# One tile of x on another DMA queue, and the bias of the hidden layer loaded and transposed earlier, in a fused linear-attention and MLP block

## The chip, the cores and the metric

The kernel runs on one core of one Trainium2 chip. The metric is device time in microseconds, the median of three runs. The names used for the core's engines are those of the profile: PE (TensorE, the matmuls) with PEld (its weight loads), DVE (VectorE), ACT (ScalarE), POOL (GpSimd) and SP (SyncE). SP does no arithmetic here: it only issues DMA transfers. ACT issues a few too, from the same instruction stream that holds its activations. "ACTq" and "SPq" mark such issues in the profile.

## The reference

The input x has 2048 tokens of 448 features. The output is x + s * g. Both factors start from the same layer norm of x:

```python
xn = _layernorm(x, axis=-1)
# linear attention, 16 heads of 28
q, k, v = split(xn @ wqkv)
phi = lambda t: jnp.where(t > 0, t + 1, jnp.exp(t)) + 1e-6
pq, pk = phi(q), phi(k)
kv = einsum("bhsd,bhse->bhde", pk, v);  z = sum over s of pk
o = (pq @ kv) / (pq . z + 1e-6)
s = o @ wo
# dense part, 448 -> 1792 -> 448
h = xn @ w1 + b1
h = relu(h) ** 2
g = silu(h @ w2 + b2)
out = x + s * g
```

All matrices are bfloat16. b1 has 1792 entries, one for each hidden unit; it is added before the relu.

## The kernel before

**Tiling.** The tokens are 16 tiles of 128, in four groups of 512. For the hidden layer the 1792 units are 14 blocks of 128: each block gives a 128 x 512 result for one group of tokens, with units on partitions, so b1 is needed with one unit per partition: a 128 x 14 tile (`b1f`). It is loaded as 14 rows of 128 (`b1r`, 3.5 KB), transposed on PE against an identity and copied out of PSUM by ACT with an ordinary activation (`bias_cols`, L1235 to L1241). The contraction length 448 is cut into three pieces of 128 and one of 64 ("rest"); the rests of two tiles or blocks share the array as halves of 64 rows.

**The order of work.** The program lists operations with what they read and write. PE and SP keep the order of the list. For ACT, DVE and POOL a planner (`one_pass`, L98) picks the next operation with durations that stand beside each operation and due times worked out from PE's order. Where a transfer has an entry in the table `landing` (L1275) the planner takes its landing time from there. The table changes no instruction by itself: it only feeds the planner, which then orders ACT, DVE and POOL for the whole program and hands out the eight PSUM banks. Semaphore waits follow from the data. Two chains of `behind` (L1264 to L1274) fix the order of the first operations on DVE (statistics of tile 0, statistics of tile 1, normalization of tile 0, and so on) and on ACT (`rs1 eT0.0 ln2 eT1.0 rs2 ln3 rs3 b1f`). An operation with a lower `prio` number is due earlier.

**The head** is the first 10 us, for token tiles 0 to 3. In words, with the names that the prediction uses:

- SP issues, in this order: x0 (tile 0 of x, L453), x1 (L454), x23 (tiles 2 and 3 together, L455), the main part of the key weights ("wk main", L456), three loads for the first 256 hidden units (w10: main and two rests, L459 to L461), b1r (L462), then the three loads of the next hidden units (w11), tiles 4 and 5 of x, w12 and so on.
- ACT first loads its function table (L452). Then it issues the two rests of the key weights ("wk rests", L457 and L458), which are made to wait for the table.
- DVE takes bn_stats and bn_aggr of a tile (L497, L498); ACT makes 1/sqrt(var + eps) out of that with Ln and Exp (L505, L509); DVE normalizes (L527, called xn0, xn1 and so on below).
- PE first multiplies a tile of zeros (`warm`, L1217, "dummies": their results are not read). It then transposes the three whole pieces of tile 0 (T0, L1246, by the code at L604), runs five dummies (L1247), transposes tile 1 (T1, L1248), two more dummies, the rests of tiles 0 and 1 (TR0, L1250), and goes on to the keys of tiles 0 and 1 (K0, K1, L803, first reader of wk main), T2, the key rests (Kr0, L818, first reader of the wk rests), T3, the first hidden blocks (L831), the rests of tiles 2 and 3 (TR2, L1258), the bias transpose (B1, L1261), and the hidden blocks' rests (Hr0, L847).
- From then on PE runs the stream of L1367 to L1383 to the end.

Of the kernel before, what the change touches and what calls it, by code (L numbers as in the profile page):

```python
# [9 lines left out]
P = 128  # L10
S, D, F = 2048, 448, 1792
# [35 lines left out]
class Program:  # L47
# [6 lines left out]
    def add(self, eng, emit, reads=(), writes=(), dur=0.2, alts=(), nbytes=0, mode=None, label="", slow=1.0):  # L54
        op = Op(eng, emit, reads, writes, dur, alts, nbytes, mode, label)
        op.slow, op.behind, op.at = slow, None, None
        for t in op.reads:
            op.raw.add(self.writer[t])
            self.readers.setdefault(t, []).append(op)
        for t in op.writes:  # L60
            w = self.writer.get(t)
            if w is not None and w is not op:
                op.deps.add(w)
            for r in self.readers.get(t, ()):
                if r is not op:
                    op.deps.add(r)
            self.writer[t] = op
            self.readers[t] = [r for r in self.readers.get(t, ()) if r is op]
        op.raw.discard(op)
        op.deps |= op.raw  # L70
        for d in op.deps:
            d.succ.append(op)
        self.ops.append(op)
        return op
# [233 lines left out]
def bass_recurrent_scan__linear_attn_block__dense_activation_squared_relu__prompt_kernel(  # L308
    nc, A_x, A_wqkv, A_wo, B_x, B_w1, B_b1, B_w2, B_b2, out
):  # L310
    with ExitStack() as es:
# [14 lines left out]
        x_tok = sb("x_tok", [P, NT, D], bf)  # L326
# [9 lines left out]
        b1r = sb("b1r", [NF, P], bf)  # L336
# [83 lines left out]
        def tiles(t, lo, hi):  # L420
            if hi <= 2:
                return t[0][P * lo : P * hi].rearrange("(p s) d -> p s d", s=1)
            base, n = (2, 2) if hi <= 4 else (lo // 4 * 4, 4)
            v = t[0][P * base : P * (base + n)].rearrange("(p s) d -> p s d", s=n)
            return v[:, lo - base : hi - base, :]

        def dma(eng, dst, src, writes, nbytes, reads=(), dur=0.45, slow=1.0):
            return add(
                eng, lambda e, _: e.dma_start(dst, src), reads, writes, dur, nbytes=nbytes, label="dma" + str(writes[0]), slow=slow
            )  # L430

        def load_x(lo, hi, eng="sp"):
            dma(eng, x_tok[:, lo:hi, :], tiles(A_x, lo, hi), [("x", i) for i in range(lo, hi)], (hi - lo) * P * D * 2)

        def load_main(eng, w, src, name, lo, hi, c0=0, c1=3, off=0):
            dma(
                eng, w[:, c0:c1, lo:hi],
                src[128 * c0 : 128 * c1, off + lo : off + hi].rearrange("(c p) j -> p c j", p=P),
                [(name, c) for c in range(c0, c1)], 128 * (c1 - c0) * (hi - lo) * 2,
            )  # L440

        def load_rest(eng, w, src, name, lo, hi, off=0, part=None):
            for i in (0, 1) if part is None else (part,):
                dma(
                    eng, w[64 * i : 64 * i + 64, 3, lo:hi], src[384:448, off + lo : off + hi], [(name, 3 + i)],
                    64 * (hi - lo) * 2, ["actw"] if eng == "act" else (), dur=0.58,
                )
# [3 lines left out]
        cuts = (0, 2 * P, 6 * P, 10 * P, F)  # L451
        add("act", lambda e, _: e.preload_act_table_set("natural_log_exp_and_others"), [], ["actw"], 1.25, label="table").prio = -1e6  # L452
        load_x(0, 1, "sp")  # L453
        load_x(1, 2, "sp")  # L454
        load_x(2, 4, "sp")  # L455
        load_main("sp", w_k, A_wqkv, "wk", 0, D, off=D)  # L456
        load_rest("act", w_k, A_wqkv, "wk", 0, D, off=D, part=0)  # L457
        load_rest("act", w_k, A_wqkv, "wk", 0, D, off=D, part=1)  # L458
        load_main("sp", w_1, B_w1, "w10", cuts[0], cuts[1])  # L459
        load_rest("sp", w_1, B_w1, "w10", cuts[0], cuts[1], part=0)  # L460
        load_rest("sp", w_1, B_w1, "w10", cuts[0], cuts[1], part=1)  # L461
        dma("sp", b1r[:, :], B_b1.rearrange("(f p) -> f p", p=P), ["b1r"], F * 2)  # L462
        for i in (1, 2, 3):
            name = f"w1{i}"
            if i == 2:
# [156 lines left out]
        def pe_transpose_rests(lo, eng):  # L622
            b = Buf("T")

            def f(e, _):
                v = ps(b)[:, :].bitcast(bf)
                for i in range(2):
                    last = e.transpose(v[:, i * P : (i + 1) * P], xn[:, lo + i, 384:512], ident[:, :])
                return last

            ts = (lo, lo + 1)
            add("pe", f, [("xd", i) for i in ts] + ["ident"], [b], 0.0558 * 2, mode="128", label=f"TR{lo}")

            def ev(e, eng):
                src = ps(b)[:, 0:P].bitcast(bf).rearrange("p (t k) -> p t k", t=2)
                if eng == "dve":
                    return e.tensor_copy(xT[:, lo : lo + 2, 3, :], src)
                return e.activation(out=xT[:, lo : lo + 2, 3, :], in_=src, func=AF.Copy)

            add(eng, ev, [b], [("xT", i) for i in ts], 0.39 if eng == "act" else 0.25, label=f"eTR{lo}").prio = -30  # L640
# [187 lines left out]
        def head_part(lo, fi):  # L828
            def f(e, _):
                for c in range(3):  # L830
                    last = e.matmul(  # L831
                        ps(head[fi])[:, lo * P : (lo + 2) * P], w_1[:, c, fi * P : (fi + 1) * P], xT[:, lo : lo + 2, c, :],
                        start=(lo == 0 and c == 0), stop=False, skip_group_check=True,
                    )
                return last

            add(
                "pe", f, [("w10", c) for c in range(3)] + [("xT", lo + i, c) for i in (0, 1) for c in range(3)] + ([head[fi]] if lo else []),
                [head[fi]], 3 * MM(256), mode="128", label=f"Ha{fi}.{lo}",
            )  # L840

        def head_rest(lo):
            fs = (lo, lo + 1)

            def f(e, _):
                for h, fi in enumerate(fs):
                    last = e.matmul(  # L847
                        ps(head[fi])[:, 0:512], w_1[half[h], 3, fi * P : (fi + 1) * P], xT[half[h], 0:4, 3, :], start=False,
                        stop=True, skip_group_check=True,
                    )  # L850
                return last

            bs = [head[fi] for fi in fs]
            add("pe", f, [("xT", i) for i in range(4)] + [("w10", 3), ("w10", 4)] + bs, bs, MM(512), mode="64", label=f"Hr{lo}")
            for fi in fs:
                h_out(head[fi], 0, fi)
# [360 lines left out]
        def warm(n, after=(), src=None):  # L1217
            b = Buf("W")

            def f(e, _):  # L1220
                last = None
                for _i in range(n):
                    last = e.matmul(ps(b)[:, 0:P], src or dum[:, 0:P], src or dum[:, 0:P], start=True, stop=True)
                return last

            add("pe", f, ["dum", *after] if src is None else [], [b], n * 0.107, mode="128", label="warm")
# [8 lines left out]
        def bias_cols():  # L1235
            bb = Buf("B1")
            add(
                "pe", lambda e, _: e.transpose(ps(bb)[:, 0 : NF // 2].bitcast(bf), b1r[:, :], ident[0:NF, 0:NF]),
                ["b1r", "ident"], [bb], 0.1, mode="128", label="B1",
            )  # L1240
            add("act", lambda e, _: e.activation(out=b1f[:, :], in_=ps(bb)[:, 0 : NF // 2].bitcast(bf), func=AF.Copy), [bb], ["b1f"], 0.2, label="b1f")  # L1241
# [2 lines left out]
        warm(30)  # L1244
        warm(4, [("mv", 0)])
        pe_transpose(0, ((0, 3, "act"),))  # L1246
        warm(5)  # L1247
        pe_transpose(1, ((0, 3, "act"),))  # L1248
        warm(2)
        pe_transpose_rests(0, "dve")  # L1250
# [3 lines left out]
        k_rests(0)  # L1254
        pe_transpose(3, ((0, 3, "dve"),))
        head_part(0, 0)
        head_part(0, 1)
        pe_transpose_rests(2, "dve")  # L1258
        head_part(2, 0)
        head_part(2, 1)  # L1260
        bias_cols()  # L1261
        head_rest(0)

        byname = {op.label: op for op in pr.ops}  # L1264
        for first, order in (
# [7 lines left out]
            if first < -26:  # L1273
                byname[names[0]].prio = first  # L1274
        landing = {  # L1275
            ("x", 0): 2.8, ("x", 1): 3.45, ("x", 2): 4.45, ("wk", 0): 6.2, ("wk", 3): 6.1, ("wk", 4): 7.6, ("w10", 0): 7.25,
            ("w10", 3): 7.55, ("w10", 4): 7.75, ("b1r", None): 7.95, ("w11", 0): 8.95, ("w11", 3): 9.2, ("w11", 4): 9.45, ("x", 4): 9.9,
            ("w12", 0): 11.2, ("w12", 3): 11.4, ("w12", 4): 11.9, ("x", 6): 13.0, ("w13", 0): 14.5, ("w13", 3): 14.8, ("w13", 4): 15.0,
        }
        for (name, k), t in landing.items():  # L1280
# [136 lines left out]
```

## Time and profile before

| What | Value |
|---|---|
| median of 3 runs | 143.62 us (143.43, 143.62, 144.87) |
| the profiled execution, its own time | 142.37 us |
| its span | 141.1 us |
| PE busy | 137.6 us, 97% of the span |
| DVE / ACT / POOL busy | 104.0 / 77.4 / 6.3 us |
| first transfer of x issued; last matmul ends | 0.81 us; 138.6 us |
| DMA engines, mean busy share in stretches of 2 us from 2 to 10 us | 0.95, 1.07, 0.92, 0.89 |

The profile is of one execution. Its span counts from the first instruction of the program to the last, and its own time is 1.27 us more. Both are below the three timed runs, so differences are worked out against the profiled execution and then carried to the median. "Busy" of PE is modelled, since matmuls are pipelined; where PE's pace matters, starts of matmuls are compared. Landing times of transfers are the last of the semaphore updates that the trace holds for a transfer.

### The profile page before, as it was taken

What the parts mean: (1) busy time and instruction counts of PE and PEld (TensorE: products, weight loads), DVE (VectorE), ACT (ScalarE), POOL (GpSimd) and SP (SyncE); (2) the same over time, 40 slices, a digit from 0 to 9 for tenths busy, and PEclk for the clock granted to TensorE, in tenths of its full rate; (3) what the DMA queues carried; (4) which work ended last, traced back from release to release, by engine and by line L of the source; (5) the groups of instructions that cost most, each with busy time, mean ns of one, the idle gap of its engine ahead of it and who ended that gap; (6) DMA issues with size and microseconds to landing.
All of it is one profiled execution on the core that took longest, in us unless ns stands there. A gap on an engine that the chain in (4) does not pass through costs nothing.

```text
span 141.1 us, 3239 instructions
## 1 busy us (share of the span) xinstructions
PE 137.6 (97%) x1299; PEld 70.9 (50%) x1299; DVE 104.0 (74%) x226; ACT 77.4 (55%) x142; POOL 6.3 (4%) x40
## 2 busy tenths in 40 slices
PE   7999999999999999999999999999999999999992
PEld 7764445454444544444444444435447455555472
DVE  1988992999798898878867799695036516874875
ACT  3759993141988526986952867696138630301312
POOL 7900000000000000000000000000000000000000
PEclk9999999999999999999999999999999999999999
DMA  4999997249923000323000000000796001223033
GB/s 98 277 289 293 312 327 147 40 61 299 178 41 52 5 0 6 50 42 47 12 5 0 0 0 5 0 0 19 183 211 133 0 0 35 96 69 102 33 98 98
DMA packets 24220, 12.91 MB, mean 91 GB/s; under 512 B 14354, under 2 KB 23566, under 8 KB 24206
## 3 DMA queue, kind: packets, MB, share of 16 engines
q1 hardware_dynamic: 22414, 11.35, 31.9%
q10 hardware_dynamic: 1792, 1.36, 4.3%
q8 instruction: 10, 0.16, 0.5%
q14 instruction: 4, 0.03, 0.1%
HBM read 9.23 MB, written 1.90 MB: 79 GB/s over the span
## 4 chain that ended last, share of the span: by engine, by line
PE 93%; DVE 3%; DMA 1%; issue 0%
PE pb L788 29%; PE pb L1094 23%; PE pb L1186 8%; PE pb L889 7%; PE pb L731 7%; PE pb L741 6%; PE pb L1111 4%; PE pb L1151 3%; DMA x_tok<-in_A_x_dram 1%; PE pb L868 1%; DVE st L497 1%; DVE gbuf L1175 1%; PE pb L895 1%; PE pb L831 1%; PE pb L1038 1%; PE pb L803 1%
## 5 line engine op out<-in xcount | busy, mean ns | idle before, releaser
L788 PE MATMUL pb<-xT,w 64*128 64x512 bf16 x378 | 43.6, 376 | 0.0
L1094 PE MATMUL pb<-w,r 64*128 64x448 bf16 x336 | 34.6, 349 | 0.0
L766 ACT ACTIVATE r<-pb,b1f 128x512 bf16<-128x512 f32 x39 | 25.2, 686 | 12.3 <-PE pb L788 12.0
L788 PEld LDWEIGHTS pb<-xT,w 64*128 64x128 bf16 x378 | 18.4, 94 | 21.7 <-DMA w<-in_B_w_dram 0.2
L1094 PEld LDWEIGHTS pb<-w,r 64*128 64x128 bf16 x336 | 16.3, 94 | 15.9 <-issue 0.4
L778 ACT ACTIVATE r<-r 128x1024 bf16<-128x1024 bf16 x15 | 15.6, 1060 | 0.1
L763 DVE TENSOR_SCALAR r<-pb,b1f 128x512 bf16<-128x512 f32 x17 | 12.4, 745 | 4.1 <-PE pb L788 3.9
L1206 DVE TENSOR_TENSOR gbuf<-pb,gbuf 128x448 bf16<-128x448 f32 x14 | 8.1, 618 | 6.6 <-PE pb L1186 6.6
L497 DVE BATCH_NORM_STATS2 st<-x_tok 128x6 f32<-128x448 bf16 x16 | 9.4, 612 | 4.7 <-DMA x_tok<-in_A_x_dram 4.7
L731 PE MATMUL pb<-w_k,xT 64*128 64x448 bf16 x98 | 11.6, 349 | 0.0
L1134 ACT ACTIVATE gbuf<-gbuf 128x448 bf16<-128x448 bf16 x14 | 7.0, 570 | 7.5 <-DVE gbuf L1084 5.9
L741 PE MATMUL pb<-xT,w_q 64*128 64x512 bf16 x84 | 11.0, 376 | 0.0
L1186 PE MATMUL pb<-w_k,pqT 64*128 64x448 bf16 x96 | 10.6, 349 | 0.0
L1084 DVE TENSOR_TENSOR gbuf<-pb,b2b 128x448 bf16<-128x448 f32 x14 | 8.0, 614 | 3.4 <-PE pb L1094 2.0
L709 ACT ACTIVATE pk<-pb 128x448 bf16<-128x448 f32 x16 | 7.8, 543 | 3.7 <-PE pb L731 3.1
L721 DVE SCALAR_TENSOR_TENSOR pk<-pb,pk 128x448 bf16<-128x448 f32 x16 | 9.6, 619 | 0.2
L889 PE MATMUL pb<-pk,xn 128*128 128x448 bf16 x48 | 9.6, 353 | 0.0
L1002 DVE TENSOR_TENSOR pqT<-pqT,xT 128x2048 bf16<-128x2048 bf16 x3 | 3.7, 1223 | 7.8 <-DMA xT<-scr 7.8
L777 DVE TENSOR_TENSOR r<-r 128x1024 bf16<-128x1024 bf16 x13 | 8.5, 684 | 0.7 <-ACT r L766 0.6
L925 DVE TENSOR_TENSOR zacc<-zacc,pk 128x448 f32<-128x448 f32 x13 | 8.0, 618 | 0.1
L709 ACT ACTIVATE pqT<-pb 128x512 bf16<-128x512 f32 x12 | 6.5, 595 | 2.2 <-PE pb L741 2.2
L721 DVE SCALAR_TENSOR_TENSOR pqT<-pb,pqT 128x512 bf16<-128x512 f32 x12 | 7.7, 682 | 0.0
(100 smaller groups left out, 131.9 us busy)
## 6 DMA issues: line engine op xcount, KB each, us to landing
w<-in_B_w_dram SPq DMA_DIRECT2D x2, 784.0 KB, 7.9
out_dram<-gbuf SPq DMA_DIRECT2D x14, 112.0 KB, 1.7
w<-in_B_w_dram SPq DMA_DIRECT2D x3, 384.0 KB, 4.7
xT<-gbuf SPq DMA_DIRECT2D x32, 32.0 KB, 2.0
x_tok<-in_A_x_dram SPq DMA_DIRECT2D x2, 448.0 KB, 5.4
x_tok<-in_A_x_dram SPq DMA_DIRECT2D x3, 224.0 KB, 3.5
xT<-scr SPq DMA_DIRECT2D x6, 112.0 KB
xT<-scr ACTq DMA_DIRECT2D x5, 112.0 KB
```

The costliest lines, as they stand in the source:

```text
L497: add("dve", lambda e, _: e.bn_stats(st6[:, si, :], x_tok[:, si, :]), [("x", si)], [("st", si)], 0.61 if si > 3 else 0.6, label=f"bn{si}") ...
L709: "act", lambda e, _: e.activation(out=slot, in_=ps(buf)[0:rows, 0:n], func=AF.Exp), [buf, "actw"],
L721: lambda e, _: e.scalar_tensor_tensor(out=slot, in0=ps(buf)[0:rows, 0:n], scalar=1.0 + 1e-6, in1=slot, op0=ALU.add, op1=ALU.max),
L731: return e.matmul(ps(b)[:, 0:D], x_tile(rows, si, c), w_k[rows, c, :], start=start, stop=stop)
L741: return e.matmul(ps(b)[:, 0:512], w_q[rows, c, m * P : (m + 1) * P], x_group(rows, g, c), start=start, stop=stop,)
L763: return e.tensor_scalar(out=slot, in0=ps(b)[:, 0:512], scalar1=b1f[:, fi : fi + 1], scalar2=0.0, op0=ALU.add, op1=ALU.max)
L766: return e.activation(out=slot, in_=ps(b)[:, 0:512], func=AF.Relu, bias=b1f[:, fi : fi + 1])
L778: return e.activation(out=both, in_=both, func=AF.Square)
L788: return e.matmul(ps(b)[:, 0:512], w_1[rows, c, fi * P : (fi + 1) * P], x_group(rows, g, c), start=start, stop=stop,)
L889: last = e.matmul(ps(b)[:, 0:D], xn_cols(si, c * P, (c + 1) * P), pk[:, si, :], start=(si == 0), stop=(si == NT - 1),)
L1094: return e.matmul(ps(b)[:, 0:D], r_cols(rows, fi, si), w_2[rows, fi, :], start=start, stop=stop)
L1186: return e.matmul(ps(b)[:, 0:D], w, msb[rows, c, :], start=start, stop=stop)
```

## The change

Four edits in the head, and new numbers in the planner's table:

1. x1 is issued by ACT ahead of its table load (its `prio` is below the table's) and no longer by SP. The two wk rests remain behind the table load.
2. b1r moves forward on SP's queue: from behind w10 to directly behind wk main.
3. On PE, B1 moves from behind the hidden blocks to between T0 and T1: the five dummies there become two, B1, two. ACT's chain is unchanged, so the copy into `b1f` still stands behind `rs3` on ACT.
4. TR2 moves forward by one hidden block of three matmuls.

```diff
-            dma(eng, x_tok[:, lo:hi, :], ...)
+            return dma(eng, x_tok[:, lo:hi, :], ...)
...
         load_x(0, 1, "sp")
-        load_x(1, 2, "sp")
+        load_x(1, 2, "act").prio = -2e6
         load_x(2, 4, "sp")
         load_main("sp", w_k, A_wqkv, "wk", 0, D, off=D)
+        dma("sp", b1r[:, :], B_b1.rearrange("(f p) -> f p", p=P), ["b1r"], F * 2)
         load_rest("act", w_k, ..., part=0)
         load_rest("act", w_k, ..., part=1)
         load_main("sp", w_1, B_w1, "w10", cuts[0], cuts[1])
         load_rest("sp", w_1, ..., part=0)
         load_rest("sp", w_1, ..., part=1)
-        dma("sp", b1r[:, :], B_b1.rearrange("(f p) -> f p", p=P), ["b1r"], F * 2)
...
         pe_transpose(0, ((0, 3, "act"),))
-        warm(5)
+        warm(2)
+        bias_cols()
+        warm(2)
         pe_transpose(1, ((0, 3, "act"),))
...
         head_part(0, 0)
+        pe_transpose_rests(2, "dve")
         head_part(0, 1)
-        pe_transpose_rests(2, "dve")
         head_part(2, 0)
         head_part(2, 1)
-        bias_cols()
         head_rest(0)
...
-            ("x", 0): 2.8, ("x", 1): 3.45, ("x", 2): 4.45, ("wk", 0): 6.2, ("wk", 3): 6.1, ("wk", 4): 7.6, ("w10", 0): 7.25,
-            ("w10", 3): 7.55, ("w10", 4): 7.75, ("b1r", None): 7.95, ...
+            ("x", 0): 2.85, ("x", 1): 3.1, ("x", 2): 4.1, ("wk", 0): 5.75, ("wk", 3): 6.1, ("wk", 4): 7.4, ("w10", 0): 7.1,
+            ("w10", 3): 7.45, ("w10", 4): 7.7, ("b1r", None): 4.9, ...
```

## The prediction

> **What bounds the kernel.** I read the page's chain that ended last, then the same chain for the first microseconds, then the waits, then the timeline of the head. The page says that PE carries the time:
>
> ```profile
> PE 137.6 (97%) x1299; PEld 70.9 (50%) x1299; DVE 104.0 (74%) x226; ACT 77.4 (55%) x142; POOL 6.3 (4%) x40
> ...
> PE 93%; DVE 3%; DMA 1%; issue 0%
> ```
>
> PE holds 93% of the chain; the rest is the head, before PE has anything to do, and the tail, which this change doesn't touch. The chain of the head, with start, length and what carried it:
>
> ```profile
> 0.81 2.11 DMA x_tok<-in_A_x_dram
> 2.92 0.02 issue
> 2.94 0.64 DVE st L497
> ...
> 3.61 0.18 DVE mv L498
> 3.79 0.52 DVE st L497
> ...
> 4.52 0.28 DVE xn L527
> 4.80 0.54 DVE st L497
> 5.34 0.35 DVE xn L527
> 5.69 0.05 issue
> 5.74 0.34 PE pb L604 x3
> ...
> 9.60 0.11 PE pb L1238
> 9.71 0.32 PE pb L847 x2
> ```
>
> x0 lands at 2.92, DVE works without a pause through to xn1, which ends at 5.69, and T1 starts on PE at 5.74. From T1 on the chain is PE alone, B1 (L1238) in it with 0.11 us. The starts of the matmuls behind agree: up to the end no gap is left that is not the pace of the stream or a change of the array's shape (some 0.1 us extra at each). So the time is the start of T1, plus what PE has to do, plus a fixed tail; one microsecond of either is one microsecond of the run.
>
> **The change part by part.** Each part is priced by what it does to T1's start or to PE's list.
>
> *x1 off SP's queue.* x1 landed at 3.26, but its bn_stats started at 3.71, on the heels of tile 0's bn_aggr: 0.45 us of cover, and DVE's order is fixed. x23 landed at 4.32 and was first read at 4.72. Landing earlier, both are worth nothing. Gain: 0.
>
> *x0 beside x1.* x0 is the first link of the chain, and now the two tiles travel together. Issues in the trace: x0 0.81 to 1.19, x1 1.25 to 1.67. From below x0 lands as now (0). From above it lands as the second of two does now, at 3.26: 0.34 later. The DMA engines' busy share is 0.86 between 2.0 and 2.25 and 0.75 up to 2.5, so there is some room but not for a whole tile. I call the delay d and take 0.15, between the two. The new table of landing times moves x0 by 0.05; it is the planner's input, not a measurement that I can look into.
>
> The Trainium skill, DMA: Bandwidth & Descriptors, section "Issuing engines are not separate DMA queues", speaks against this edit: transfers started by different engines run on the same 16 DMA engines and interleave, so starting on two at once saves only the time to start them. By that rule d would be near its upper end; this trace has no two loads started together on idle engines, so it can't settle it (rival C).
>
> *ACT's side.* An issue of 128 rows takes 0.42 on SP, one of 64 rows 0.59 to 0.61 on ACT; so the table load (1.28) and the wk rests come 0.46 to 0.64 later:
>
> ```profile
> 0.80 1.28 ACT L452 ACT_TABLE_LOAD   x1 [0.80 <-PEq L1402]
> 2.12 1.23 ACTq L429 DMA_DIRECT2D w_k<-in_A_wqkv_dram  x2
> 3.82 0.29 ACT L505 ACTIVATE vep<-mv,eps 128x1 f32<-128x1 f32 x1 [1.74 <-POOL hm L415]
> ```
>
> ACT stood idle from 3.34 to the first Ln at 3.82, so the issues now end at 3.81 to 3.98 and Ln starts up to 0.2 late. xn0 waited for bn_aggr of tile 1 rather than ACT by 0.05, and d shifts it too, so I charge nothing beyond d (0 to 0.15). The second wk rest landed at 7.18; Kr0 read it at 7.55. That cover of 0.36 us is about what the issue loses, and T1's own delay adds to it. Charge 0; without cover at most 0.1 to 0.3.
>
> *SP's queue.* Without x1 everything behind it is issued 0.46 earlier, x23 and wk main first. b1r (0.61 and 0.04 to the next) then puts w10 0.19 later than now, and from w11 on the lead is 0.46 again. w10 main landed at 7.09 and is read at 8.02: 0.9 of cover. The last of w11 landed at 9.65 and PE's weight load took it at 9.69: no cover now, so without the lead a faster head would wait there. It comes earlier, and PE is not much earlier: 0.
>
> *B1 out of PE's path.* B1 started at 9.54 and Hr0 at 9.65; without B1, Hr0 starts after its own change of shape:
>
> ```profile
> 9.53 0.09 PEld L1238 LDWEIGHTS pb<-ident,b1r 14*128 14x128 bf16 x1 [0.21 <-issue]
> 9.54 0.18 PE L1238 MATMUL pb<-ident,b1r 14*128 14x14 bf16 x1
> 9.64 0.10 PEld L847 LDWEIGHTS pb<-xT,w 64*128 64x128 bf16 x2
> 9.65 0.39 PE L847 MATMUL pb<-xT,w 64*128 64x512 bf16 x2
> ```
>
> Start to start from the last hidden matmul (9.33) to B1 is 0.205, to Hr0 another 0.109; the hidden matmuls step by 0.109. So taking B1 out saves 0.109. In the dummies it costs nothing if b1r is there: T0's three and two dummies end at about 5.2, B1 with two changes of shape takes 0.2, two dummies 0.11, and T1 can't start before 5.74.
>
> *B1 waits for b1r.* This is the new wait. It stands in PE's order ahead of T1 and of everything else. b1r is issued 2.20 us after the start. From below: as quickly as x0 on idle engines, 2.11 from issue: 4.3. From above: behind wk main where that lands now, 6.05 plus 0.20: 6.25. The 0.20 is from b1r's own row: it now lands at 7.79, and the load ahead of it in SP's queue at 7.58. That is the nearest row, since it is this transfer on this queue, and it says that b1r doesn't overtake. wk main is issued 0.46 earlier but shares the engines with x0 and x1; I take 5.6 for it, and with 0.1 behind it **b1r at 5.7** (the table assumes 4.9; no row gives that to a transfer behind 336 KB on the same queue). The engine starts a weight load 0.04 after a landing (w11: 9.65 to 9.69); B1 and two dummies take 0.22. So T1 starts at 5.70 + 0.27 = 5.97, 0.23 after now, and d up to 0.23 is hidden in that.
>
> *The copy into b1f* (0.18) goes to ACT behind `rs3`, which ended at 7.28; ACT then idled 0.67. At its old place ACT idled 0.82 before it and the relu waited for Hr0 anyway. 0 both ways. B1's PSUM bank is held until about 7.5, when four or five of eight are in use.
>
> *TR2 earlier*: same instructions, same shape; its input was done at 8.11 and it now runs at about 8.35. 0.
>
> **The sum**: T1 0.23 later, B1's 0.109 less: +0.12 us. On the profiled execution: span 141.1 to 141.2, own time 142.37 to 142.5. The median stands 1.25 above that; carried over, 143.62 to **143.7**.
>
> **The rivals.**
>
> A. *b1r is in time.* If it lands by 5.47 + d, T1 is where x0 puts it, and the net is d - 0.11: -0.11 with d = 0, +0.04 with 0.15. Time 143.5 to 143.65. For it: it is 3.5 KB, one row each for 14 of the 16 engines (14 of its landing updates came with data), so it needn't wait for the slowest engine. Against it: b1r's own row. Chance 0.30.
>
> B. *b1r holds PE for longer.* PE's list stops at B1, and with it T1, TR0, K0 and all that follows. The net is the landing minus 5.58: it decides from there. At 5.9 it is +0.32, at 6.25 +0.67: 143.9 to 144.3. For it: wk main's queue is full, engine shares 1.0 to 1.1 from 3.5 to 6. Against: wk main is issued 0.46 earlier. Chance 0.12.
>
> C. *x0 and x1 share evenly.* d = 0.34, T1 at 6.08, net +0.23: 143.85. For it: the engines' share in 2.0 to 2.5. Against: x1's descriptors may start later, since ACT's queue gave its first packets 2.4 us after its first issue, SP's 1.0. Chance 0.12. The section of the Trainium skill named above would make the run this case.
>
> D. *Another plan.* The planner orders ACT and DVE anew for the whole program. PE has no stall left to lose, so it can only get worse: a stall like the longest PE waits now, 0.2 to 0.4 each, up to some five of them. The nearest point is the attention's scaling: DVE ends it at 113.3, PE reads it at 114.4, so 1.1 us of delay there are free. Net +0.2 to +2. Chance 0.08.
>
> That x1 would not go ahead of the table is out: it waits for nothing and has the lower number. Were it issued behind the table, at 2.12 instead of 1.25, it would land at about 4.1 and bn_stats of tile 1 would wait 0.4.
>
> **How the numbers follow.** The forecast has the remaining 0.38, with a range of its own of 143.6 to 143.9. A to C lie between 143.5 and 144.3. Three runs lay between 143.43 and 144.87, so a median moves by some tenths without cause: I give 143.0 to 144.4. One per cent is 1.44 us, about what a measurement of this kernel tells from no change. No term gains that: faster 0.03, for the runs' spread. Slower, 0.06, needs the upper part of D or a disturbed median. Same: 0.91.
>
> **What the profile will show.** b1r's landing, B1's start on PE and what PE waited for there (this decides between the forecast, A and B); x0's landing against 2.92 (C); the first Ln on ACT, 3.8 to 4.0; T1 at about 5.97; Hr0's start against T1's, 3.80 instead of 3.91; no PE wait for w11; and behind 10 us the same PE pace as now (D). The prediction is wrong if T1 starts before 5.7, or if PE gains gaps behind the head.

## The result, and the profile after

The changed kernel took 144.44 us in the median of 22 executions (143.13 to 145.48), the kernel before 143.53 (142.89 to 144.87): a ratio of 1.006 with a 95% interval of 1.0032 to 1.0089. By the medians it is slower by about 0.9 us, less than one per cent. The median hides that the executions fall into two groups: 11 of 22 lie between 143.13 and 144.00, and 11 between 144.89 and 145.48. On another chip 8 of 12 lay between 142.74 and 143.74 and 4 between 145.01 and 145.16. There the kernel before had a median of 143.08. A ratio leaves out executions more than 1.5% above the fastest: two of the long ones in the first comparison, and all four on the other chip, where it is 1.000 (0.9982 to 1.0019). So the median of the 22 is a middle at which no execution lies: the lower group alone has a median of 143.54, the upper one of 145.25.

The profiled execution after is one of the lower group: 143.19 us, span 142.0, against 142.37 and 141.1 before. The page has as much PE work as before; in the chain DMA has 3% instead of 1%, and SP's issues (SPq) are new:

```profile
PE 137.5 (97%) x1298; PEld 70.5 (50%) x1298; DVE 104.1 (73%) x226; ACT 77.3 (54%) x142; POOL 6.7 (5%) x40
...
PE 93%; DMA 3%; DVE 1%; SPq 1%; issue 0%
```

The chain of the head, with start, length and what carried it:

```profile
1.71 0.44 SPq L429
2.15 0.04 issue
2.20 4.22 DMA b1r<-in_B_b_dram
6.42 0.05 issue
6.46 0.18 PE pb L1238
6.64 0.22 PE pb L1223 x2
6.86 0.17 PE pb L604 x3
...
10.54 0.32 PE pb L847 x2
```

x0 and DVE are gone from the chain. In their place stands the transfer of b1r, 4.22 us for 3.5 KB, and B1 (L1238) behind it, then T1. The timeline of the same stretch shows what each engine waited for (the bracket is the idle time before, and what ended it):

```profile
3.32 0.63 DVE L497 BATCH_NORM_STATS2 st<-x_tok 128x6 f32<-128x448 bf16 x1 [2.32 <-DMA x_tok<-in_A_x_dram]
...
4.20 0.29 ACT L505 ACTIVATE vep<-mv,eps 128x1 f32<-128x1 f32 x1 [1.67 <-DVE mv L498]
...
5.42 0.28 PE L1223 MATMUL pb<-dum 128*128 128x128 bf16 x2
...
6.46 0.18 PE L1238 MATMUL pb<-ident,b1r 14*128 14x14 bf16 x1 [0.78 <-DMA b1r<-in_B_b_dram]
...
6.70 0.33 PE L604 MATMUL pb<-ident,xn 128*128 128x128 bf16 x3
```

The first bn_stats starts at 3.32 instead of 2.94, because x0 landed at 3.29 instead of 2.92. xn1 was ready at 6.06, but PE stood at B1 from its two dummies (start of the last: 5.47) to 6.46. T1 starts at 6.70 instead of 5.74 (+0.96), Hr0 at 10.48 instead of 9.65 (+0.83, since B1 no longer stands ahead of it), and the last matmul ends at 139.44 instead of 138.61 (+0.83). Behind the head PE's starts have the same gaps as before, at the same places.

So the two profiled executions differ by 0.8 us, and the wait for b1r accounts for it. It doesn't explain the upper group, whose median is 1.7 us above the lower one's (2.0 on the other chip). Nor does it agree with the lower group, whose median of 143.54 is that of the kernel before, 143.53; more on that at the end. The experiments went after what delays b1r and x0, and what the upper group is.

### The profile page after: what moved, and what is told of

The parts are those of the page before. It is cut to its first block, busy times and chain, and to the rows that moved or that the text cites. A ratio compares the mean times of both kernels' runs of the same rounds, so it can differ in the third digit from the quotient of the medians.

```text
span 142.0 us, 3238 instructions
## 1 busy us (share of the span) xinstructions
PE 137.5 (97%) x1298; PEld 70.5 (50%) x1298; DVE 104.1 (73%) x226; ACT 77.3 (54%) x142; POOL 6.7 (5%) x40
## 4 chain that ended last, share of the span: by engine, by line
PE 93%; DMA 3%; DVE 1%; SPq 1%; issue 0%
PE pb L788 29%; PE pb L1094 22%; PE pb L1186 7%; PE pb L889 7%; PE pb L731 7%; PE pb L741 6%; PE pb L1111 4%; PE pb L1151 3%; DMA b1r<-in_B_b_dram 3%; PE pb L868 1%; DVE gbuf L1175 1%; PE pb L895 1%; PE pb L831 1%; PE pb L1038 1%; SPq L429 1%; PE pb L803 1%
```

## The experiments

Each run was timed beside the kernel before on its chip: median 142.92 (29 executions) for the first four runs, 143.08 (35) for the next four, 142.99 (28) for the last four. None of these 92 executions of the kernel before was above 144.32; in the first comparison one of its 22 was (144.87). "Late" below means an execution above 144.6 us; the changed kernel had 15 late ones in 34. The groups of four ran on three different chips, and the changed kernel itself was timed again only beside the second group.

### B1 back at its old place

```diff
-        warm(2)
-        bias_cols()
-        warm(2)
+        warm(5)
...
         head_part(2, 1)
+        bias_cols()
```

> The changed kernel with one edit undone: the bias transpose B1 is back behind the hidden blocks, and five dummies stand between T0 and T1. x1 stays on ACT's queue, b1r stays behind wk main on SP's. Theory 1 (B1 waits for b1r, and PE's pause of about 1 us there also costs the full clock in some executions): B1 no longer waits; T1 is set by x0, which landed 0.37 later in the changed kernel, so T1 at about 6.1 and Hr0 0.3 to 0.45 later than in the kernel before; about +0.4 us, and all runs close together. Rival (the transfers started together are the whole loss): as slow as the changed kernel, +0.8 or more, whatever PE does.

Median 143.03 in 11 executions, 142.68 to 143.30, ratio 0.9992 (0.9971 to 1.0013), none late. T1 was at 6.09, as expected from x0 (landed at 3.33). Then came something not expected: K0 waited for wk main. From the chain:

```profile
1.71 5.01 DMA w_k<-in_A_wqkv_dram
6.72 0.14 issue
6.85 1.29 PE pb L803 x6
```

wk main was issued at 1.71, 0.47 earlier than in the kernel before, and landed at 6.72, 0.67 later. Hr0 came 0.70 later than in the profile before, and yet the median rose by only 0.1 us, where 0.4 was expected. With B1 out of the way no execution was late, as theory 1 has it; with B1's wait two of 12 were on the same chip (next run). That the median rose so little needs another reason; the clock (below) is the likely one.

### x1 back on SP's queue

```diff
-        load_x(1, 2, "act").prio = -2e6
+        load_x(1, 2, "sp")
```

> The changed kernel with x1 back on SP's queue behind x0; b1r stays behind wk main and B1 among the dummies. Theory 1: b1r still can't land before wk main, which landed at 6.05 in the kernel before: b1r at 6.0 to 6.4, B1 waits for it, T1 at about 6.4; x0 lands at 2.9 again; Hr0 +0.5 us, with runs that are about 2 us longer still present if PE's pause decides them. Rival (x1 on ACT is the whole loss): T1 back at 5.74 and the time 0.1 us below the kernel before.

Median 143.30 in 12, 143.00 to 144.87, two of them late; ratio 1.0042 (1.0016 to 1.0068).

```profile
2.67 3.60 DMA b1r<-in_B_b_dram
6.27 0.05 issue
6.32 0.18 PE pb L1238
```

x0 landed at 2.90 again and wk main at 6.06, but b1r behind it at 6.27. T1 was at 6.55 and Hr0 at 10.33, +0.69. The rival falls: with x1 where it was, B1 still waits, and b1r landed 0.21 after the 336 KB ahead of it.

### Dummies for the pause

```diff
-        warm(2)
+        warm(20)
         bias_cols()
```

> The changed kernel with 20 dummies instead of 2 ahead of B1, so that PE works (1.0 us of dummies at full clock) while b1r is on its way; nothing else differs. If PE's pause is what makes some executions 2 us longer (the clock is granted or kept only while PE is busy): T1 and Hr0 as in the changed kernel's profile, +0.8 to +0.9 us, and no run above about 144.1. Rival (in those executions b1r or x0 lands 2 us later): as many long runs as before, since dummies move no transfer.

> The changed kernel with 20 dummies ahead of B1 once more, since the first look had only five executions. Theory: no execution 2 us above the rest, so the highest stays below 144.3; the median +0.4 to +0.7 us against the kernel before. Rival: 4 in 10 of them above 144.7.

The first of these two runs had five executions, 143.45 to 143.84, median 143.58, ratio 1.0046 (1.0034 to 1.0058). The second had 12, 143.36 to 144.14, median 143.51, ratio 1.0040 (1.0024 to 1.0056). None of the 17 was late. Ten dummies instead of twenty:

> The changed kernel with 10 dummies instead of 2 ahead of B1. They shorten PE's pause from 1.0 us to about 0.5 at full clock, and leave none at half clock. Theory (the pause decides whether the full clock is granted in time): T1 as in the changed kernel, and clearly fewer executions 2 us above the rest than its 15 of 34. Rival (late transfers make them): the share stays near 15 of 34.

11 executions, 143.12 to 144.30, median 143.50, ratio 1.0042 (1.0025 to 1.0059), none late. From its timeline, PE hardly pauses before B1:

```profile
5.55 1.10 PE L1223 MATMUL pb<-dum 128*128 128x128 bf16 x10
6.83 0.18 PE L1238 MATMUL pb<-ident,b1r 14*128 14x14 bf16 x1 [0.18 <-DMA b1r<-in_B_b_dram]
```

In the three profiles b1r landed as late as in the changed kernel or later (6.44, 7.02 and 6.79), and T1 came later still (7.35, 7.64, 7.07), but of 28 executions none was late, where 15 of 34 were. Dummies move no transfer, so neither late transfers nor a late T1 make the upper group; what the dummies took away is PE's idle time. One limit: the changed kernel itself was not timed beside these runs; on the chip of the first five, two of 12 were late with B1's wait (the run before); on the chip of the other 23 only the longest execution of the run with the pause filled bears on it (below). The next run makes the pause alone, on the chip where four of 12 executions of the changed kernel were late.

### A pause in the kernel before, and nothing else

```diff
-        warm(5)
+        warm(5, [("wk", 0)])
```

> The kernel before with one edit: the five dummies between T0 and T1 wait for wk main (landed at 6.05), so PE pauses for about 0.95 us where the changed kernel does, and no transfer and no instruction is moved. T1 at 6.37 instead of 5.74, Hr0 +0.63 us. Theory (PE's pause costs the clock in some executions): some executions 1.5 to 2 us above the rest, as in the changed kernel. Rival (the moved transfers make them): one close group at about +0.6 us.

Median 143.21 in 12, ratio 1.0035 (1.0005 to 1.0065). Nine lay between 142.95 and 143.69 and three at 144.78 to 144.83. So the pause alone makes late executions. The other nine have a median of 143.09, the kernel before 143.08: for them the pause cost nothing that shows. The profiled execution was a late one (144.83, span 143.6), and its timeline shows what happens:

```profile
4.74 0.53 PE L604 MATMUL pb<-ident,xn 128*128 128x128 bf16 x3
6.00 0.71 PE L1223 MATMUL pb<-dum 128*128 128x128 bf16 x5 [0.73 <-DMA w_k<-in_A_wqkv_dram]
6.51 0.53 PE L604 MATMUL pb<-ident,xn 128*128 128x128 bf16 x3
...
7.25 2.45 PE L803 MATMUL pb<-w_k,xT 128*128 128x448 bf16 x6
9.49 0.53 PE L604 MATMUL pb<-ident,xn 128*128 128x128 bf16 x3
...
10.26 0.34 PE L604 MATMUL pb<-ident,xn 128*128 128x128 bf16 x3
```

A transpose of three pieces takes 0.53 up to 9.5 and 0.34 from 10.26 on. K0 and K1 take 2.45 us; in the kernel before they took 1.30:

```profile
6.15 1.30 PE L803 MATMUL pb<-w_k,xT 128*128 128x448 bf16 x6
```

The trace records the clock that PE is granted, in these runs either full or half. PE runs at half pace until about 10.0, where the first such record grants the full clock: at 10.02. In the kernel before that record stands at 5.01. The page's row of the granted clock shows full speed for the whole span in both, since nothing is recorded ahead of the first grant; the pace of the matmuls has to be read instead. From T1 to Hr0 it took 5.56 us instead of 3.91: 1.65 more, which with the 0.77 by which T1 was late is the 2.42 by which Hr0 and the span grew.

In eleven other traces with such a record, from kernels with and without a pause, the grant came between 4.51 and 6.83. The full-clock stretches that begin with it are 133.12, 136.53 and 139.95 us long in the twelve traces: 39, 40 and 41 steps of 3.41. Half pace through one such step costs half of it, 1.71 us. That is close to the 1.65 here, to the 1.70 between the medians of this run's two groups and to the 1.71 between those of the changed kernel in the first comparison (2.0 on the other chip). So a late execution looks like one that is a step of full clock short.

The Trainium skill, TensorE: Matmul & The Clock Gate, Part 1, says that the full clock is given after a busy window of about 3.4 us and that the windows run freely, not from the kernel's start. The traces agree as far as they go: the stretches above differ by 3.41, and in this run the pause ended at 6.00 and the grant came 4.0 us later.

### The pause filled

```diff
-        warm(5)
+        warm(18)
+        warm(5, [("wk", 0)])
```

> The run with the pause (the kernel before, five dummies between T0 and T1 waiting for wk main) with 18 more dummies ahead of that wait, so that PE works until wk main has landed. T1 at 6.4 as with the pause, or up to 0.5 later where the dummies run at half clock. Theory: the executions 2 us above the rest, 3 of 12 with the pause, are gone; +0.1 to +0.5 us. Rival (the late T1, not the idle PE, makes them): 3 of 12 again.

Six executions, 144.24 to 147.16, median 145.13, ratio 1.0135 (1.0102 to 1.0169). This run doesn't answer its question. T1 came at 6.29 at full pace, but then:

```profile
10.07 0.18 PE L1238 MATMUL pb<-ident,b1r 14*128 14x14 bf16 x1
12.19 0.39 PE L847 MATMUL pb<-xT,w 64*128 64x512 bf16 x2 [1.94 <-DVE xT L637]
```

Hr0 waited 1.94 us for the eviction of TR2 on DVE, which ran at 11.86 behind the statistics of tile 4 (11.31, waiting for x):

```profile
11.31 0.63 DVE L497 BATCH_NORM_STATS2 st<-x_tok 128x6 f32<-128x448 bf16 x1 [2.20 <-DMA x_tok<-in_A_x_dram]
11.86 0.27 DVE L637 COPY xT<-pb 128x256 bf16<-128x256 bf16 x1
```

In the kernel before this eviction came first (8.99, the statistics at 10.18). The only edit is the dummies, so it is the planner that turned the order round. It is rival D of the prediction, met in an experiment. The case against late transfers rests on the other fill runs. The longest execution here, 147.16, is 2.0 above the median and has a mean granted clock of 0.988, as some late ones of the changed kernel have (below); its kernel too has a PE wait early on.

### x1 alone on ACT's queue

```diff
-        load_x(1, 2, "sp")
+        load_x(1, 2, "act").prio = -2e6
```

(the kernel before, nothing else changed)

> The kernel before with only x1 moved to ACT's queue, ahead of the table load; b1r and B1 stay where they were. Theory: x0 lands at 3.2 to 3.4 instead of 2.9, T1 at 6.05 to 6.15, wk main no earlier than before, Hr0 0.3 to 0.4 later in the profile; no execution 2 us above the rest; in the median less than that, 0 to +0.3 us, since the full clock is often granted later than T1 anyway. Rival (SP's lead of 0.46 is worth something): not slower than the kernel before in the profile.

Median 143.29 in 12, 142.76 to 143.41, none late; ratio 1.0015 (1.0001 to 1.0029).

```profile
0.81 2.49 DMA x_tok<-in_A_x_dram
...
3.32 0.64 DVE st L497
...
6.14 0.27 PE pb L604 x3
...
10.07 0.32 PE pb L847 x2
```

x0 landed at 3.30 instead of 2.92, T1 came at 6.07, Hr0 at 10.00 instead of 9.65: +0.36, about x0's delay of 0.38. x1 itself landed at 3.49, later than the 3.26 from SP's queue, and wk main at 6.22 instead of 6.05, though issued 0.47 earlier. So this edit by itself loses in the profile what x0 loses, and 0.2 to 0.3 us in time.

### b1r with nothing ahead of it

```diff
-        dma("sp", b1r[:, :], ...)
+        dma("act", b1r[:, :], ...).prio = -2e6
...
-        warm(5)
+        warm(2)
+        bias_cols()
+        warm(2)
```

(the kernel before; x1 stays on SP's queue, ACT issues b1r ahead of the table load, B1 leaves its old place)

> The kernel before with b1r issued by ACT ahead of its table load instead of by SP, and B1 among the dummies as in the change; x1 stays on SP's queue. b1r then has no load ahead of it on its queue: it lands by about 3.3, B1 doesn't wait, T1 at 5.74 as in the kernel before, and Hr0 0.109 earlier. Against it: the table load and the wk rests come 0.5 to 0.6 later; a wk rest then lands at up to 7.7 and Kr0, which read it at 7.55, would wait up to 0.2. Expected net between -0.11 and +0.1 us. Rival (B1 in the dummies costs PE by itself, through its two changes of shape): T1 later than 5.8 with b1r there.

b1r landed at 2.68 and B1 never waited. But the table load and the two wk rests came 0.7 later:

```profile
0.81 0.66 ACTq L429 DMA_DIRECT2D b1r<-in_B_b_dram  x1
1.50 1.28 ACT L452 ACT_TABLE_LOAD   x1 [1.50 <-PEq L1403]
2.81 1.21 ACTq L429 DMA_DIRECT2D w_k<-in_A_wqkv_dram  x2
4.13 0.29 ACT L505 ACTIVATE vep<-mv,eps 128x1 f32<-128x1 f32 x1 [1.35 <-POOL zmask L391]
```

The issues ended at 4.03 and the first Ln started at 4.13 instead of 3.82. (The releaser named is a POOL memset of a tile that Ln doesn't read; of its inputs, eps was written by 1.57 and bn_aggr ended at 3.74.) xn0 then waited for ACT, T1 came at 6.03, Hr0 at 9.83, +0.18. B1 among the dummies wasn't the reason: it ran at 5.54, and T1 waited for xn1. Median 142.83 in 12, ratio 1.0004 (0.9988 to 1.0020). The wait that was expected at Kr0 did not come; the price was at Ln.

Two variants tried to keep ACT free. From POOL:

> The kernel before with b1r issued by POOL behind its first constants instead of by SP, and B1 among the dummies as in the change; x1 stays on SP's queue and ACT's stream is as before. If b1r lands by about 5.2, B1 doesn't wait, T1 is at 5.74 as before, Hr0 0.109 earlier, and w11 comes 0.65 earlier: -0.1 us. If the transfer from POOL takes over 3.7 us to land, B1 waits as in the changed kernel: +0.3 or more.

b1r landed at 4.18 and B1 didn't wait. But x1, issued on SP's queue at 1.27 while POOL issued b1r from 1.32 on, landed at 4.00 instead of 3.26, and its bn_stats now waited for it:

```profile
4.02 0.63 DVE L497 BATCH_NORM_STATS2 st<-x_tok 128x6 f32<-128x448 bf16 x1 [0.40 <-DMA x_tok<-in_A_x_dram]
```

T1 was at 6.17. The full clock came at 6.53, so T1 ran at half pace. Median 142.89 in 12, ratio 1.0001 (0.9977 to 1.0026). And with one wk rest given to SP's queue in b1r's old stead:

> As the run with b1r on ACT ahead of the table load, but the second wk rest goes to SP's queue, behind wk main, so that ACT issues two transfers as before and is free for the first Ln by 3.5. There the first Ln had come at 4.13 instead of 3.82, which made T1 0.29 later. Expected: b1r by 2.7, first Ln at about 3.8, T1 at 5.74 to 5.8, Hr0 0.1 earlier than in the kernel before: -0.1 us. If Ln stays late, the issues on ACT were not what delayed it.

This did to the head what the change was to do: b1r at 2.64, the first Ln at 3.72, T1 at 5.62, Hr0 at 9.42, 0.22 earlier than before. The next matmul then waited:

```profile
9.42 0.39 PE L847 MATMUL pb<-xT,w 64*128 64x512 bf16 x2
10.37 0.39 PE L788 MATMUL pb<-xT,w 64*128 64x512 bf16 x2 [0.56 <-DMA w<-in_B_w_dram]
```

The last rest of w11 landed at 10.33, 0.68 later than in the kernel before; why is open. Median 143.21 in 12, ratio 1.0019 (1.0000 to 1.0038). So here w11's landing, and not the head, set what follows. Had it landed at 9.65 as before, this matmul could have started at about 9.7 instead of 9.87, by an estimate from the 0.04 between landing and start here; that a faster head has nothing to hand on is not shown. No version here beat the kernel before by more than its interval.

### The changed kernel once more

> The changed kernel itself, unedited, on the chip of this comparison, as the measure for the others. Expected from its first 22 executions: times in two groups, about 143.1 to 144.0 and 144.9 to 145.5 minus what this chip is quicker, with roughly half in the upper one. Theory (the clock): in the upper group PE runs some 3.4 us longer at half clock, which costs up to 1.7 us, either because the full clock is granted a window later or because it is taken back. Rival (transfers): the upper group shows the usual clock and a later b1r.

Median 143.29 in 12, four of them late. Its profiled execution was again one of the lower group, with x0 at 3.22, wk main at 6.17, b1r at 6.41 and T1 at 6.69. There is no trace of a late one, so that their half pace looks like that of the run with the pause is inferred. What is there is the mean granted clock: 1.000 or 0.999 in every one of the lower group, and 0.988 in two of the four late ones (0.987 or 0.988 in seven of eleven in the first comparison). A mean that is 0.012 short over 144 us stands for 3.5 us at half clock, about one step of 3.41. At most 0.4 us of that can lie at the end, since in the twelve traces the full clock lasts until 2.1 us or more after the last matmul and the span ends 2.5 us after it. So in these the clock seems to have been granted and then taken back for a step. In the other late ones nothing is missing after the first grant, as in the run with the pause, where the grant itself was late.

## Why the prediction came out as it did

The mechanism that it priced was right: B1 waited for b1r, and everything behind it on PE came later. The verdict by one per cent was right too. The sum of +0.12 us was far too small: between the two profiles the same wait cost 0.83. That the median fell so near the range is luck. 144.44 lies 0.04 above its upper end (143.93, without the two longest executions, inside), and it is the middle between two groups, one of them with the median of the kernel before and one 1.7 above. The 0.9 us between the medians comes from the late executions, for which the prediction has no term, and not from the wait at the price that it gave. By its steps:

- **B1 waits for b1r: right, and mis-sized.** The step put b1r at 5.7, from above at 6.25; it landed at 6.42. The term that failed is the one below it, "I take 5.6 for wk main": that assumed that an earlier issue lands earlier. wk main landed at 6.62, 0.57 later than before. In the seven traces with x1 on ACT it landed at 6.17 to 6.92, in the seven with x1 on SP at 5.68 to 6.06, although it is issued 0.47 later there. Why is open: the 16 updates of one landing spread over 1.8 us in the changed kernel (4.85 to 6.62) and over 1.0 before, so a few of the engines' shares come late. That b1r doesn't get clear of the load ahead was right: in the seven traces with it behind wk main it landed between 0.20 ahead of it and 0.24 behind.
- **Rival B was the case, and its formula held between the profiles,** for a landing beyond its bound. Landing minus 5.58 gives 0.84 for 6.42; Hr0 and the end of PE came 0.83 later.
- **x0 beside x1: the upper bound.** d was taken as 0.15, from above 0.34; it was 0.37, and x0 landed at 3.22 to 3.36 in all seven traces. That is rival C. The rule of the Trainium skill quoted in the prediction, that two issuing engines save only issue time, is what these traces show: x1's landing gained nothing (3.42 to 3.54 from ACT, 3.26 in the kernel before). In the changed kernel d was hidden behind b1r; x1's edit alone shows it.
- **B1 out of PE's path: right.** Hr0 starts 0.205 after the last hidden matmul.
- **ACT's side: right for this change.** The first Ln started at 4.20, on the heels of its own input at 4.16; the second wk rest landed at 8.05 and Kr0 ran at 8.48. The run with b1r on ACT showed that the cover there is small: issues that end at 4.03 with x0 on time do cost.
- **w11: no PE wait, as forecast.** It landed at 9.99 and was read at 10.70. PE waited for it only in the run with the faster head, where it also landed 0.68 later than before.
- **TR2, the copy into b1f, PSUM: nothing seen.** No new PE gap behind the head, so rival D did not occur in this kernel.
- **What was missed is the clock.** The wait was priced at its length, one for one. In 15 of 34 executions it cost 1.7 to 2.0 us more, and that is the whole of the measured difference: the lower groups have medians of 143.54 and 143.06, the kernel before 143.53 and 143.08.

That last pair leaves a question: the profiles differ by 0.8, the lower groups hardly at all. The profile before, with 142.37, is quicker than all 22 timed executions of the kernel before in that comparison, and its grant at 5.01 is ahead of T1. A later grant costs a kernel that starts T1 at 5.74 more than one that starts it at 6.70, since less of the real work is run at half pace. The grants of 5.3 to 6.8 in other traces fit this, and several runs show the same gap between profile and median: Hr0 +0.70 and median +0.1 with B1 back, +0.48 and -0.2 with b1r on POOL's queue, +1.78 and +0.5 with twenty dummies, and no change in the nine that were not late with the pause. It was not measured for the kernel before itself, of which there is one trace, so the reason is argued and not shown.

## What to carry to other kernels

An operation moved into idle time on an engine that keeps its order, as PE does here, brings its input's landing time with it, and everything behind it on that engine inherits the wait: check when the input lands on its queue, behind what stands ahead of it, not when it is issued. Issuing on a second queue made two loads finish together here rather than the first one early; if a chain starts from the first, keep the second behind it. And in the first microseconds, when PE is still being brought to full clock, a pause was priced here by what it did to the clock, not by its length: fill it, or don't create it.

## What the runs showed of the hardware that was not expected

- A PE pause of 0.7 to 1.0 us between 5.3 and 6.5 us costs a step of 3.41 us of full clock in part of the executions. In the one that was traced the grant came at 10.02 instead of 4.5 to 6.8, and K0 and K1 took 2.45 us instead of 1.30. 15 of 34 executions with b1r's wait, 2 of 12 with that wait and x1 back on SP's queue, and 3 of 12 with a bare pause were 1.5 to 2.0 us longer in the median than the others of their run; none of 28 with the pause shortened or filled was, and one of 114 of the kernel before.
- Two tiles of 112 KB issued at the same moment on two queues landed at 3.29 and 3.47; issued 0.44 us apart on one queue they landed at 2.92 and 3.26. The later one gained nothing and the first lost 0.37.
- A transfer of 3.5 KB behind 336 KB on its queue took 4.22 us to land; issued first on ACT's queue it took 1.87 (0.81 to 2.68).
